# Two of six projection chunks computed as a 2x2 block product in seven products over pairs of rows

## The chip, the cores and the metric

The kernel runs on one core of a Trainium2 chip. The metric is the device time of one execution in microseconds, the median of several runs. The core's engines are named as in the profile: PE (TensorE, the matmuls), DVE (VectorE), ACT (ScalarE), POOL (GpSimd) and SP (SyncE, which here only issues DMA transfers). Each engine works through its own instructions in the order in which the kernel wrote them; a semaphore holds an instruction, and all behind it on that engine, until what it needs is there.

## The reference

Two mixers are computed from the same x (2048 rows of 1024) and blended by a gate. One is a local attention with 32 heads of 32, in which each position looks at eight positions, two apart; the other is a gated MLP with a product along the sequence.

```python
def reference(A_x, A_wqkv, A_wo, B_x, B_w_in, B_w_sp, B_b_sp, B_w_out, gate_w):
    x = A_x
    g = _sigmoid((x * gate_w).sum(-1, keepdims=True))
    a = _A_ref(x, A_wqkv, A_wo)                        # sliding, dilated attention
    b = _B_ref(x, B_w_in, B_w_sp, B_b_sp, B_w_out)     # gated MLP
    return g * a + (1 - g) * b

# _A_ref: qkv = x @ wqkv                      (1024 x 3072)
#         idx = pos - 2 * [0..7]; logits = q . k[idx] / sqrt(32), masked where idx < 0
#         a = (softmax(logits) . v[idx]) @ wo
# _B_ref: z = gelu(x @ w_in)                  (1024 x 3584), z1, z2 = its halves
#         z2 = layernorm(z2);  g = w_sp @ z2 + b_sp;  b = (z1 * g) @ w_out
```

Inputs and output are bfloat16.

## The kernel before

All work stands in one program order, written out by hand, under a manual schedule. PE's matmuls carry the time, and the other engines' work is put between them. A small planner (`Beat`) keeps a nominal clock, advanced by `beat.run(columns)` after every group of matmuls; `beat.at(t, fn)` puts other work into the program when the nominal clock reaches t, and the attention's DVE steps (`attention_steps(t)`) are drawn one after the other as the planner thinks DVE free. So the order on each engine is fixed when the program is built; only waits are decided on the chip.

The stages in order are:

- The first quarter of z2 (`z2_quad`, `z2_tile(i, 0)`), 128 rows by 512 columns at a time. Each tile is eight matmuls into one of eight PSUM banks, and ACT applies the gelu.
- The QKV projection. The weights' 24 blocks of 128 columns (8 groups of heads times q, k, v) make six chunks of four blocks (`wg_slots`, two slots in turn). Per chunk there are 16 "rows" j: row j holds the 128 positions p x 16 + j. A row is eight matmuls of 512 columns (`L520`), a copy of the bank by ACT (`L523`) and, for every four rows, four stores (`store_rows`, one per block) to q_d, k_d or v_d in DRAM. Chunk 0 is done as two halves of 256 columns. For blocks of v the weight columns are put in another order by ACT (`v_order`, `L269`, 1024 elements a partition). The loads of a chunk come a chunk ahead (`load_wg`).
- While PE works on the projection and what follows, DVE does the attention: per group a multiply of q by shifted k (`L326`, 8192 elements, twice a group), folds (`L329`, `L332` and so on), `soft_a`, the exponential on ACT (`soft_exp`, `L356`), `soft_b`, and the products with v (`L369` to `L376`).
- The rest of z2. The last of each row's tiles has one more column, the gate's weight, loaded at `L492`; the statistics and the norm of z2 and the gates follow.
- z1 (`L595`), then two chunks of the product along the sequence (`g_chunk`, `L613`), then the rest of it as 2x2 block products in seven products (`seven_products`, `L704`), which need sums of weight blocks (`t_sums`, `s_sum`).
- The output products (`mix_pair`, `attn_pair`, `both_pairs`), also in seven products.

The products in seven use f16 sums, and the factors are scaled by a power of two first, so that the sums fit. The power is found by `whole_power`: the largest absolute values (ACT's Abs with a sum on the way, or a DVE reduction) are rounded to a power on DVE and written to `top_b`; PE transposes this column to a row (`L557`); DVE reduces it to one number, `top_1`; PE spreads that over all partitions by a matmul (`L560`); six small DVE operations make the power and its inverse. Each `next(steps)` writes the part up to the next `yield`.

The projection's loop before is:

```python
    for ch in range(NCH):
        wgt = wg_slots[ch % 2]
        for pos0, pos1 in ((0, 2), (2, 4)) if ch == 0 else ((0, 4),):
            n0, n1 = pos0 * C, pos1 * C
            for j in range(NJ):
                if j == 4 and 0 < ch and ch + 1 < NCH:
                    load_wg(ch + 1)
...
                if j == 8 and pos1 == 4 and ch + 1 < NCH:
                    v_order(ch + 1)
```

Of the kernel before, what the change touches and what calls it, by code (L numbers as in the profile page):

```python
# [36 lines left out]
W2P = FH + 32  # L37
# [12 lines left out]
ARENA = EF_OFF + 15360  # L50
# [7 lines left out]
def kernel(  # L58
# [24 lines left out]
    def reg(off, n):  # L83
        return arena[:, off:off + n]
# [6 lines left out]
    wsp_d = dpool.tile([8, P, S], BF, name="wsp_d")  # L91
    wo_d = dpool.tile([NG, P, D], BF, name="wo_d")
# [4 lines left out]
    def warm_up(widths):  # L97
        pw = psum.tile([P, 512], F32, name="pw", tag="ps")
        for n in widths:
# [25 lines left out]
    v_l1 = sm.tile([P, 28], F32, name="v_l1")  # L125
# [9 lines left out]
    w_up = sm.tile([P, 1], I32, name="w_up")  # L135
    u_up = sm.tile([P, 1], I32, name="u_up")
# [19 lines left out]
    w2 = reg(CD_OFF, KT * W2P).rearrange("p (k c) -> p k c", k=KT)  # L156
    stage_slots = [reg(off, 2048).rearrange("p (j c) -> p j c", j=4)
                   for off in (CD_OFF + 14592, CD_OFF + 16640, EF_OFF + 13056)]
    wg_slots = [reg(EF_OFF + r * WGS, WGS).rearrange("p (t k c) -> p t k c", t=4, k=KT) for r in range(2)]
    vraw_slots = [reg(EF_OFF + 2 * WGS + r * KT * C, KT * C).rearrange("p (k c) -> p k c", k=KT) for r in range(3)]  # L160
    junk = reg(EF_OFF + 2 * WGS + 3 * KT * C, FH)
# [89 lines left out]
    def blocks(ch):  # L251
        return BLOCKS[4 * ch:4 * ch + 4]

    def load_w(ch, pos):
        g, part = blocks(ch)[pos]
        dst = vraw_slots[g % 3] if part == 2 else wg_slots[ch % 2][:, pos, :, :]
        sync.dma_start(dst, wq_v[:, :, part * D + g * C:part * D + (g + 1) * C])
# [5 lines left out]
    def v_order(ch):  # L263
        for pos, (g, part) in enumerate(blocks(ch)):
            if part != 2:
                continue
            vdst = wg_slots[ch % 2][:, pos, :, :].rearrange("p k (d h) -> p k d h", d=DH, h=HG)
            vsrc = vraw_slots[g % 3].rearrange("p k (h d) -> p k d h", h=HG, d=DH)
            nc.scalar.copy(vdst, vsrc)  # L269
# [9 lines left out]
    def z2_mm(ps, i, c, kt, N):  # L279
        nc.tensor.matmul(ps[:, 0:N], xT[:, kt, i * P:(i + 1) * P], w2[:, kt, ZC * c:ZC * c + N],  # L280
                         start=(kt == 0), stop=(kt == KT - 1))
# [100 lines left out]
    def load_v(g):  # L382
        sync.dma_start(v_t, bass.AP(tensor=v_d.tensor, offset=v_d.offset + (g * (S + 16) + 2) * C, ap=[[NJ * C, P], [1, NJJ * C]]))
# [10 lines left out]
    def attention_steps(t):  # L394
        beat.at(t - 8.0, lambda: load_qk(0))
        beat.at(t + 35.0, lambda: load_v(0))
# [75 lines left out]
    tc_order = ctx.enter_context(tc.manual_schedule())  # L472

    for i in range(2):
        sync.dma_start(xn[:, i, :], x_v[:, i, :])  # L475
    for c in range(2):
        sync.dma_start(w2[:, 0, ZC * c:ZC * (c + 1)], win_v[:, 0, FH + ZC * c:FH + ZC * (c + 1)])  # L477
    for kt in range(1, KT):
        sync.dma_start(w2[:, kt, 0:2 * ZC], win_v[:, kt, FH:FH + 2 * ZC])  # L479
    for i in range(2, 16):  # L480
        if i == 14:
            load_w(0, 0)
            load_w(0, 1)
        sync.dma_start_transpose(xT[:, :, i * P:(i + 1) * P], x2[i * P:(i + 1) * P, :])
    load_w(0, 2)
    load_w(0, 3)
    load_wg(1)
    for t_d in (k_d, v_d):
        sync.dma_start(bass.AP(tensor=t_d.tensor, offset=t_d.offset, ap=[[16, P], [(S + 16) * C, NG], [1, 16]]), zeros[:])
    for c in range(2, 4):  # L490
        sync.dma_start(w2[:, :, ZC * c:ZC * c + ZW[c]], win_v[:, :, FH + ZC * c:FH + ZC * c + ZW[c]])
    sync.dma_start(w2[:, :, FH:FH + 1], gw_v)  # L492

    warm_up((512,) * 6 + (128,))
    z2_quad()
    for i in range(2, 16):
        z2_tile(i, 0)

    QK_US = NJ * KT * 2 * C * BEAT
    beat.steps = attention_steps(beat.now + QK_US + 10.0)  # L500

    stg = 0
    def store_rows(st, ch, j0, pos0, pos1):
        for pos in range(pos0, pos1):
            g, part = blocks(ch)[pos]
            t_d, rows, first = ((q_d, S, 0), (k_d, S + 16, 16), (v_d, S + 16, 16))[part]
            dst = bass.AP(tensor=t_d.tensor, offset=t_d.offset + (g * rows + first + j0) * C, ap=[[NJ * C, P], [C, 4], [1, C]])
            sync.dma_start(dst, st[:, :, pos * C:(pos + 1) * C])

    for ch in range(NCH):  # L510
        wgt = wg_slots[ch % 2]
        for pos0, pos1 in ((0, 2), (2, 4)) if ch == 0 else ((0, 4),):
            n0, n1 = pos0 * C, pos1 * C
            for j in range(NJ):
                if j == 4 and 0 < ch and ch + 1 < NCH:
                    load_wg(ch + 1)
                ps = psum.tile([P, 512], F32, name="ps", tag="ps")
                for kt in range(KT):
                    lhsT = _sub_ap(xT_flat, kt * S + j, [[NJ, P]])
                    nc.tensor.matmul(ps[:, n0:n1].rearrange("p (t c) -> p t c", c=C), lhsT, wgt[:, pos0:pos1, kt, :],  # L520
                                     start=(kt == 0), stop=(kt == KT - 1))
                st = stage_slots[stg % 3]
                nc.scalar.copy(st[:, j % 4, n0:n1], ps[:, n0:n1])  # L523
                if j % 4 == 3:
                    store_rows(st, ch, j - 3, pos0, pos1)
                    stg += 1
                if j == 8 and pos1 == 4 and ch + 1 < NCH:
                    v_order(ch + 1)
                beat.run(KT * (n1 - n0))

    load_w1(0)
    load_w1(1)
    sync.dma_start(b_row[:], bass.AP(tensor=B_b_sp.tensor, offset=B_b_sp.offset + 1024, ap=[[P, 8], [1, P]]))
    for i in range(16):
        for c in range(2 if i < 2 else 1, 4):
            z2_tile(i, c)
        nc.scalar.activation(junk.rearrange("p (f q) -> p f q", q=P), z2[:, :, i, :], ACT.Square, accum_out=s2[:, i:i + 1])
        if i % 4 == 3:
            beat.at(beat.now + 6.0, lambda i=i: stats(i))
            for ii in range(i - 3, i + 1):  # L540
                beat.at(beat.now + 11.0, lambda ii=ii: norm(ii))
    beat.at(beat.now + 8.0, gates)
    for aa in range(4):
        beat.at(beat.now + 8.0 + 6.0 * aa, lambda aa=aa: load_wsp(0, aa))
    beat.at(beat.now + 6.0, lambda: sync.dma_start(
        bsp_bc[:, 0:1024], bass.AP(tensor=B_b_sp.tensor, offset=B_b_sp.offset, ap=[[0, P], [1, 1024]])))

    def whole_power(up1, factors):
# [19 lines left out]
        yield  # L568

# [424 lines left out]
    def extra(n, place):  # L994
# [14 lines left out]
        if n == 5 and place == 0:  # L1009
            nc.vector.tensor_reduce(top[:], v_l1[:], AX.X, ALU.max)  # L1010
            next(v_steps)
# [102 lines left out]
```

## Time and profile before

| what | value |
|---|---|
| median of 3 runs | 691.0 us (690.73 to 691.04) |
| the profiled execution | 691.45 us, of which the span is 689.4 |
| PE busy | 683.3 us, 99% of the span |
| DVE, ACT busy | 530.3 us (77%), 385.9 us (56%) |
| first quarter of z2 | to 38.35 us |
| projection, L520 | 38.35 to 204.44 us, 896 matmuls |
| rest of z2 | to 270.30 us |
| z1 | to 367.00 us |
| g_chunk, twice | to 465.50 us |
| seven_products | to 551.60 us |
| granted TensorE clock | 1.000 |

The times of the stages are those of PE in the profiled execution, counted from the start of the span. A group of the profile is named by its line in the kernel, engine, operation and tiles, with the count of its instructions, their busy time and the mean duration of one, and then the idle time of the engine ahead of them with what ended it. Matmuls overlap, so that the time from one to the next is shorter than the duration of one. In a timeline each row has its start, its duration, and in brackets the idle time of that engine before it. PE is idle for about 6 us in all, none of it in the projection.

### The profile page before, as it was taken

What the parts mean: (1) busy time and instruction counts of PE and PEld (TensorE: products, weight loads), DVE (VectorE), ACT (ScalarE), POOL (GpSimd) and SP (SyncE); (2) the same over time, 40 slices, a digit from 0 to 9 for tenths busy, and PEclk for the clock granted to TensorE, in tenths of its full rate; (3) what the DMA queues carried; (4) which work ended last, traced back from release to release, by engine and by line L of the source; (5) the groups of instructions that cost most, each with busy time, mean ns of one, the idle gap of its engine ahead of it and who ended that gap; (6) DMA issues with size and microseconds to landing.
All of it is one profiled execution on the core that took longest, in us unless ns stands there. A gap on an engine that the chain in (4) does not pass through costs nothing.

```text
span 689.4 us, 9052 instructions
## 1 busy us (share of the span) xinstructions
PE 683.3 (99%) x3355; PEld 359.1 (52%) x3355; DVE 530.3 (77%) x685; ACT 385.9 (56%) x778; POOL 12.6 (2%) x44
## 2 busy tenths in 40 slices
PE   8999999999999999999999999999999999999998
PEld 3489666666665555444444444444444444444443
DVE  0003779999999999999999887276589998766653
ACT  4345444345458898764675987853665552222332
POOL 0000000000000111000000000000000000000000
PEclk9999999999999999999999999999999999999999
DMA  8996769678856213998988938937112433222210
GB/s 225 181 217 171 145 196 229 129 168 194 200 159 200 88 58 117 245 214 295 320 264 224 356 128 195 245 95 267 39 32 62 128 56 86 68 62 61 70 54 30
DMA packets 186411, 108.14 MB, mean 157 GB/s; under 512 B 145920, under 2 KB 171008, under 8 KB 186112
## 3 DMA queue, kind: packets, MB, share of 16 engines
q1 hardware_dynamic: 184064, 99.18, 55.1%
q10 hardware_dynamic: 2304, 8.39, 3.1%
q8 instruction: 26, 0.43, 0.2%
q14 instruction: 17, 0.14, 0.1%
HBM read 59.25 MB, written 34.15 MB: 135 GB/s over the span
## 4 chain that ended last, share of the span: by engine, by line
PE 98%; DMA 1%; SPq 0%; ACT 0%; DVE 0%; issue 0%; DVEq 0%
PE ps L520 24%; PE ps L613 14%; PE ps L595 14%; PE ps L280 14%; PE ps L704 12%; PE ps L830 12%; PE ps L919 6%; PE ps L909 1%; DMA arena<-in_B_w_in_dram 1%; PE po L560 0%; SPq L477 0%; SPq L475 0%; PE po L557 0%; ACT arena L973 0%; DVE arena L899 0%; SPq L479 0%
## 5 line engine op out<-in xcount | busy, mean ns | idle before, releaser
L520 PE MATMUL ps<-arena 128*128 128x512 bf16 (+1 forms) x896 | 166.2, 349 | 0.0
L520 PEld LDWEIGHTS <-arena 128*128 128x128 bf16 x896 | 120.2, 144 | 45.9
L326 DVE TENSOR_TENSOR arena<-arena 128x8192 bf16<-128x8192 bf16 x16 | 70.8, 4422 | 57.4 <-DMA arena<-k_d 57.2
L523 ACT CAST arena<-ps 128x512 bf16<-128x512 f32 (+1 forms) x112 | 57.7, 526 | 85.2 <-PE ps L520 79.5
L280 PE MATMUL ps<-arena 128*128 128x512 bf16 (+1 forms) x512 | 97.6, 352 | 2.1 <-DMA arena<-in_B_w_in_dram 2.1
L613 PE MATMUL ps<-arena 128*128 128x512 bf16 x448 | 97.7, 379 | 0.0
L595 PE MATMUL ps<-arena 128*128 128x512 bf16 x448 | 96.9, 379 | 0.0
L830 PE MATMUL ps<-arena 128*128 128x512 f16 (+1 forms) x392 | 92.8, 379 | 0.0
L704 PE MATMUL ps<-arena 128*128 128x512 bf16 (+1 forms) x392 | 85.5, 379 | 0.0
L280 PEld LDWEIGHTS <-arena 128*128 128x128 bf16 x512 | 50.1, 98 | 49.3 <-issue 2.7
L369 DVE TENSOR_TENSOR arena<-arena,att_A 128x8192 bf16<-128x8192 bf16 x16 | 70.7, 4419 | 2.7 <-DMA arena<-v_d 2.7
L595 PEld LDWEIGHTS <-arena 128*128 128x128 bf16 x448 | 43.8, 98 | 52.7
L613 PEld LDWEIGHTS <-arena 128*128 128x128 bf16 x448 | 43.3, 98 | 52.3 <-issue 0.7
L830 PEld LDWEIGHTS <-arena 128*128 128x128 f16 (+1 forms) x392 | 38.3, 98 | 46.1
L704 PEld LDWEIGHTS <-arena 128*128 128x128 bf16 (+1 forms) x392 | 38.0, 98 | 45.9 <-issue 0.5
L329 DVE TENSOR_TENSOR arena<-arena 128x4096 bf16<-128x4096 bf16 (+1 forms) x32 | 56.2, 1758 | 1.0
L919 PE MATMUL ps<-arena 128*128 128x512 f16 (+3 forms) x200 | 50.3, 375 | 0.0
L285 ACT ACTIVATE arena<-ps 128x512 bf16<-128x512 f32 (+1 forms) x64 | 34.3, 538 | 28.3 <-PE ps L280 28.3
L899 DVE SCALAR_TENSOR_TENSOR arena<-ps,g_s,arena 128x512 bf16<-128x512 f32 (+2 forms) x33 | 23.9, 733 | 28.5 <-ACT arena L951 20.0
L598 ACT ACTIVATE arena<-ps 128x512 bf16<-128x512 f32 x56 | 30.7, 596 | 17.3 <-DMA z_d<-arena 11.6
L375 DVE TENSOR_TENSOR arena<-arena 128x4096 bf16<-128x4096 bf16 x16 | 36.6, 2289 | 0.3
L919 PEld LDWEIGHTS <-arena 128*128 128x128 f16 (+1 forms) x200 | 19.4, 98 | 23.1 <-issue 0.2
(169 smaller groups left out, 624.0 us busy)
## 6 DMA issues: line engine op xcount, KB each, us to landing
arena<-k_d SPq DMA_DIRECT2D x8, 960.0 KB, 6.5
arena<-v_d SPq DMA_DIRECT2D x8, 960.0 KB, 9.3
arena<-in_A_wqkv_dram SPq DMA_DIRECT2D x24, 256.0 KB, 4.5
z_d<-arena SPq DMA_DIRECT2D x12, 512.0 KB, 7.5
arena<-in_B_w_in_dram SPq DMA_DIRECT2D x4, 1024.0 KB, 7.5
q_d<-arena SPq DMA_DIRECT2D x32, 128.0 KB, 2.7
k_d<-arena SPq DMA_DIRECT2D x32, 128.0 KB, 2.4
arena<-q_d SPq DMA_DIRECT2D x8, 512.0 KB, 4.3
```

The lines of the kernel that those rows point to most:

```text
L280: nc.tensor.matmul(ps[:, 0:N], xT[:, kt, i * P:(i + 1) * P], w2[:, kt, ZC * c:ZC * c + N], start=(kt == 0), stop=(kt == KT - 1))
L326: TT(prod.rearrange("p (w j c) -> p w j c", w=W, j=8, c=C), in0, in1, ALU.mult)
L329: return lambda: TT(pv[:, :, 0:half], pv[:, :, 0:half], pv[:, :, half:2 * half], ALU.add)
L369: TT(prod.rearrange("p (w j d h) -> p w j d h", w=W, j=8, d=DH, h=HG), in0, in1, ALU.mult)
L375: return [(4.4, mul), (2.3, lambda: TT(p3[:, 0:4, :], p3[:, 0:4, :], p3[:, 4:8, :], ALU.add)), (1.2, lambda: TT(p3[:, 0:2, :], p3[:, 0:2, ...
L520: nc.tensor.matmul(ps[:, n0:n1].rearrange("p (t c) -> p t c", c=C), lhsT, wgt[:, pos0:pos1, kt, :], start=(kt == 0), stop=(kt == KT - 1))
L523: nc.scalar.copy(st[:, j % 4, n0:n1], ps[:, n0:n1])
L595: nc.tensor.matmul(ps[:], w1[:, kt, (f % 4) * P:(f % 4 + 1) * P], xT[:, kt, 512 * c:512 * (c + 1)], start=(kt == 0), stop=(kt == KT - 1))
L613: nc.tensor.matmul(ps[:], z2[:, f, i, :], wsp[:, i, :, :].rearrange("p a t -> p (a t)"), start=(i == 0), stop=(i == 15))
L704: nc.tensor.matmul(dst[:], lhs[:, k, :], rhs(k), start=first and k == 0, stop=k == 7, skip_group_check=not first)
L830: nc.tensor.matmul(dst[:], lhs[:, j, :], rhs(j), start=first and j == 0, stop=j == 6, skip_group_check=not first)
L919: nc.tensor.matmul(dst, lhs[:, k, :], rhs[:, k, :], start=first and k == 0, stop=k == 3, skip_group_check=not first)
```

## The change

Chunks 3 and 4 (eight blocks, 1024 columns) are taken together as a 2x2 block product: the two block rows of x are the positions of rows j = 2m and 2m + 1, the inner dimension is halved (four tiles of 128 each), and the weight's halves are b11, b21 (chunk 3) and b12, b22 (chunk 4). `row_pair(m, ...)` makes two rows of both chunks in seven products of four matmuls (28 instead of 32), in Winograd's form, with the partial sums held in PSUM, copied from bank to bank by ACT, and joined by two DVE operations a pair. Between its products stand the eight matmuls of one row of chunk 5 in three parts (`plain_rows(5, m, 0, 4, 2, 3)`). The order of the chunks becomes 0, 1, 2, the eight pairs with rows 0 to 7 of chunk 5, rows 8 to 15 of chunk 5.

The sums that this needs are made as follows.

- Sums of x: `x_sum` finds the largest absolute values of x on DVE during the first quarter of z2; `x_steps` (a `whole_power`) is put at rows 3 and 6 of the first half of chunk 0; `x_block_sums` at row 7 makes `a22s` on ACT and five arrays of 4096 elements on DVE, ahead of the attention, in the part of z2's memory that isn't yet written. The second row block of z2's tiles that lies there is stored to `z2_d` and loaded again after the pairs.
- Sums of the weights: the loads of chunks 3, 4 and 2 are issued after chunk 0, chunk 5's after chunk 1. In chunk 1 ACT finds the weights' sizes (`q_abs`, 16 Abs of 512 elements, rows 5 to 12) and reorders v blocks (rows 4, 7, 9); `q_first_step` is at row 14, and the other two steps of `q_steps` at rows 0 and 2 of chunk 2. There follow `q_scale` (rows 3 to 6, ACT), `v_order(5)` (row 7), four `q_sum` (row 9, DVE) and two scalings by the power of x (rows 11 and 12).

Chunk 2's weights lie where w2's first quarter was, so the loads of w2's last two quarters, of the gate column and the loading of z2 from `z2_d` come after the pairs. The attention is planned 3 us later (13.0 in place of 10.0 behind the first half of chunk 0), and `t_sums` and `s_sum` 4 us earlier. A pair's rows are stored two at a time, in place of four.

The diff, cut to its core:

```diff
+    def x_sum(i):
+        v = xn[:, i, :] if i < 2 else xT[:, :, i * P:(i + 1) * P]
+        nc.vector.tensor_reduce(x_l1[:, i:i + 1], v, AX.X if i < 2 else AX.XY, ALU.max,
+                                apply_absolute_value=True)
...
+    def x_block_sums():
+        v = nc.vector
+        nc.scalar.activation(a22s, x_block(1, 1), ACT.Copy, scale=x_by)
+        v.tensor_scalar(a21s, x_block(0, 1), x_by, None, ALU.mult)
+        TT(x_sums[0], a22s, a21s, ALU.add)
+        v.scalar_tensor_tensor(x_sums[2], x_block(0, 0), x_by, a21s, ALU.mult, ALU.subtract)
+        v.scalar_tensor_tensor(x_sums[1], x_block(0, 0), x_by, x_sums[0], ALU.mult, ALU.subtract)
+        v.scalar_tensor_tensor(x_sums[3], x_block(1, 0), x_by, x_sums[1], ALU.mult, ALU.add)
+
+    def q_abs(k):
+        slot = wg_slots[3 + k // 8]
+        nc.scalar.activation(abs_out.rearrange("p (k c) -> p k c", k=4), slot[:, k % 8 // 2, 4 * (k % 2):4 * (k % 2) + 4, :],
+                             ACT.Abs, accum_out=q_l1[:, k:k + 1])
+
+    def q_scale(ch, h, up1):
+        v = wg_slots[ch][:, 2 * h:2 * h + 2]
+        nc.scalar.activation(v, v, ACT.Copy, scale=up1[:].bitcast(F32))
...
+    def q_first_step():
+        nc.vector.tensor_reduce(top[:], q_l1, AX.X, ALU.max)
+        next(q_steps)
...
-    beat.steps = attention_steps(beat.now + QK_US + 10.0)
+    beat.steps = attention_steps(beat.now + QK_US + 13.0)
...
+    def row_pair(m, filler):
...
+        pa = bank()
+        mm(pa, plain(0), b11, True)
+        pb = bank()
+        nc.scalar.copy(pb[:], pa[:])
+        pe = bank()
+        mm(pe, summed(x_sums[0]), t_w[0], True)
+        act(e5, pe[:], ACT.Copy, scale=back1)
+        next(filler)
+        mm(pb, summed(x_sums[1]), t_w[1], False)
+        pc = bank()
+        nc.scalar.copy(pc[:], pb[:])
+        mm(pa, plain(1), b21, False)
+        act(st3[:, 0, :], pa[:], ACT.Copy, scale=back1)
+        next(filler)
+        mm(pb, summed(x_sums[2]), t3_w, False)
+        pd = bank()
+        nc.scalar.copy(pd[:], pb[:])
+        stt(st4[:, 1, :], pb[:], back1, e5, ALU.mult, ALU.add)
+        beat.on_vector(0.75)
+        mm(pc, summed(x_sums[3]), b22, False)
+        stt(st4[:, 0, :], pc[:], back1, e5, ALU.mult, ALU.add)
+        beat.on_vector(0.75)
+        next(filler)
+        mm(pd, lambda k: a22s[:, k, m:1024:8], t_w[2], False)
+        act(st3[:, 1, :], pd[:], ACT.Copy, scale=back1)
+        for st, ch in ((st3, 3), (st4, 4)):
+            store_rows(st, ch, j, 2, 0, 4)
...
+    for pos0, pos1 in ((0, 2), (2, 4)):
+        for j in range(NJ):
+            if pos0 == 0 and j in (3, 6):
+                next(x_steps)
+            if pos0 == 0 and j == 7:
+                x_block_sums()
+            if pos0 == 2 and j == 2:
+                v_order(1)
+            run_all(plain_rows(0, j, pos0, pos1))
+    for ch in (3, 4, 2):
+        load_wg(ch)
+    for j in range(NJ):
+        if j in (4, 7, 9):
+            v_order({4: 3, 7: 4, 9: 2}[j])
+        if 5 <= j < 13:
+            q_abs(2 * j - 10)
+            q_abs(2 * j - 9)
+        if j == 14:
+            q_first_step()
+        run_all(plain_rows(1, j, 0, 4))
+    load_wg(5)
+    for j in range(NJ):
+        if j in (0, 2):
+            next(q_steps)
+        if 3 <= j < 7:
+            q_scale(3 + (j - 3) // 2, (j - 3) % 2, q_up)
+        if j == 7:
+            v_order(5)
+        if j == 9:
+            for k in range(4):
+                q_sum(k)
+        if j in (11, 12):
+            q_scale(3, j - 11, x_up)
+        run_all(plain_rows(2, j, 0, 4))
+    for m in range(8):
+        row_pair(m, plain_rows(5, m, 0, 4, 2, 3))
+    for c in (2, 3):
+        sync.dma_start(w2[c][:, :, 0:ZW[c]], win_v[:, :, FH + ZC * c:FH + ZC * c + ZW[c]])
+    sync.dma_start(w2[3][:, :, 256:257], gw_v)
+    sync.dma_start(z2[:, 4:8, 0:2, :], z2_d[:])
+    stg[0] = 0
+    for j in range(8, NJ):
+        run_all(plain_rows(5, j, 0, 4))
...
-        beat.at(t0 + 82.0 + 2.5 * k, lambda k=k: t_sums(k))
+        beat.at(t0 + 78.0 + 2.5 * k, lambda k=k: t_sums(k))
...
-        beat.at(t0 + 87.0 + 0.8 * k, lambda k=k: s_sum(0, k))
+        beat.at(t0 + 83.0 + 0.8 * k, lambda k=k: s_sum(0, k))
```

In the changed kernel `whole_power`'s transpose is L498 and its matmul L501, and the projection's matmuls are L612 (rows) and L632 (pairs).

More of the change, by code (lines that the diff above doesn't have):

```diff
@@ L500 @@
-    beat.steps = attention_steps(beat.now + QK_US + 10.0)
[L502 to L546, printed above, removed]
     def whole_power(up1, factors):
@@ new lines, with x_block @@
+    for i in range(2, 16):
+        x_sum(i)
+        z2_tile(i, 0)
+        if i == 8:
+            sync.dma_start(z2_d[:], z2[:, 4:8, 0:2, :])
+    nc.vector.tensor_reduce(top[:], x_l1, AX.X, ALU.max)
+    x_steps = whole_power(x_up, q_back[:])
+    next(x_steps)
+    x_by = x_up[:].bitcast(F32)
+    def x_block(half, e):
+        return x_even_odd[:, 4 * half:4 * half + 4, :, e]
+    def x_block_sums():
[6 more added lines that the diff above has]
+        v.scalar_tensor_tensor(x_sums[3], x_block(1, 0), x_by, x_sums[1], ALU.mult, ALU.add)
@@ L1009, in extra @@
         if n == 5 and place == 0:
-            nc.vector.tensor_reduce(top[:], v_l1[:], AX.X, ALU.max)
+            nc.vector.tensor_reduce(top[:], v_l1, AX.X, ALU.max)
             next(v_steps)
```

169 lines of the change are left out of this document (130 added, 39 removed).

## The prediction

> **What bounds the kernel now.** I read the page's busy times, the chain that ended last and the groups first. PE is busy for 99% of the span and the chain is PE; L520, the projection that is changed, is its largest line, and PE never waits for another engine in it.
>
> ```profile
> PE 683.3 (99%) x3355; PEld 359.1 (52%) x3355; DVE 530.3 (77%) x685; ACT 385.9 (56%) x778; POOL 12.6 (2%) x44
> PE 98%; DMA 1%; SPq 0%; ACT 0%; DVE 0%; issue 0%; DVEq 0%
> L520 PE MATMUL ps<-arena 128*128 128x512 bf16 (+1 forms) x896 | 166.2, 349 | 0.0
> L523 ACT CAST arena<-ps 128x512 bf16<-128x512 f32 (+1 forms) x112 | 57.7, 526 | 85.2 <-PE ps L520 79.5
> ```
>
> So a matmul less is a gain at full price, and a wait of PE a loss at full price. Next the timeline of ACT over the second chunk (columns: start, duration, engine, line, operation, count, idle before):
>
> ```profile
> 76.75 0.58 ACT L523 CAST arena<-ps 128x512 bf16<-128x512 f32 x1 [1.15 <-PE ps L520]
> 78.48 0.58 ACT L523 CAST arena<-ps 128x512 bf16<-128x512 f32 x1 [1.14 <-PE ps L520]
> ...
> 82.41 3.85 ACT L269 COPY arena<-arena 128x1024 bf16<-128x1024 bf16 x2
> 86.12 1.60 ACT L523 CAST arena<-ps 128x512 bf16<-128x512 f32 x3
> 87.73 1.28 ACT L356 ACT_TABLE_LOAD   x1
> 89.03 0.63 ACT L356 ACTIVATE att_L<-att_L 128x512 f32<-128x512 f32 x1
> ```
>
> Row copies come every 1.7255 us (mean over the rows), so one of the row's 8 matmuls takes 215.7 ns. A copy behind other work holds ACT 0.485, one v_order 1.92. For each row ACT has 1.14 us free and no more. The price of an Abs with its sum is 0.755 from start to start, 0.70 to a copy behind it, in a later stage of the same timeline:
>
> ```profile
> 381.55 0.63 ACT L633 ACTIVATE arena<-arena 128x512 bf16<-128x512 bf16 x1
> 382.08 0.19 ACT L633 ACTIVATION_READ_ACCUMULATOR arena<-arena 128x1 f32 x1
> 382.31 0.63 ACT L633 ACTIVATE arena<-arena 128x512 bf16<-128x512 bf16 x1
> ```
>
> DVE around the first softmax, where it waits for ACT once:
>
> ```profile
> 89.69 0.42 DVE L347 TENSOR_TENSOR att_m<-att_L 128x256 f32<-128x256 f32 x1 [6.26 <-ACT att_L L356]
> ...
> 91.94 4.42 DVE L326 TENSOR_TENSOR arena<-arena 128x8192 bf16<-128x8192 bf16 x1
> 96.39 2.29 DVE L329 TENSOR_TENSOR arena<-arena 128x4096 bf16<-128x4096 bf16 x1
> ```
>
> And PE: what a broadcast matmul and a transpose of whole_power cost it between others, and the start of the kernel:
>
> ```profile
> 0.77 2.83 PE L100 MATMUL pw<-const-bfloat16-1.0 128*128 128x512 bf16 x7 [0.77 <-PEq L1098]
> 3.38 1.35 PE L296 MATMUL pt<-ident,arena 128*128 128x128 bf16 x16
> ...
> 401.94 0.38 PE L560 MATMUL po<-top,const-bfloat16-1.0 1*128 1x512 bf16 x1
> 402.26 1.04 PE L613 MATMUL ps<-arena 128*128 128x512 bf16 x4
> ```
>
> The profiled execution took 691.45 us, its span 689.4; the median of the runs is 691.0. My terms are differences on its timeline, and I add them to the median.
>
> **Saving.** Sixteen rows of two chunks were 256 matmuls; eight pairs of 7 products of 4 are 224. 32 x 215.7 ns = -6.90 us. The f16 products are priced like bf16: both have a mean of 379 ns in their groups.
>
> **Added on PE.** Two whole_powers. The matmul costs 402.26 - 401.94 = 0.32; a transpose at 498.42 had the next matmul at 498.57, 0.15. Together +0.94. The first one's parts are before chunk 1 (+0.47).
>
> **The x part.** Sixteen tensor_reduce on DVE lie beside the first z2 tiles, where DVE is idle (its first multiply is at 62.25); I take them as hidden: the transpose is two us behind the last. x_block_sums starts near 45; its ACT half, 4096 elements, is 3.7 us at the rate of L670 (2048 in 2.0, contiguous) or 7.7 at L269's (1024 in 1.92, strided), against eight banks of 0.873 us = 7.0. So 0 to 1.3; I take 0, as the banks have part of it free.
>
> **Chunk 1, the main term.** All of q_abs (16 Abs) and v_order(3), (4) and twice (2) now stand in ACT's order in rows 4 to 12 of chunk 1. Row 3's copy starts at 73.30 + 0.47 = 73.77 and frees ACT at 74.25. Behind it: v_order(3) 1.92, the copy of row 4 0.485, eight times two Abs (0.755 + 0.70) with seven copies (0.485) between, 15.0, v_order(4) 1.92, v_order(2) 3.84: 23.2 us, in which nothing waits. The last Abs ends at A = 97.4. PE, which has eight banks, isn't held (the copies lag by 8 us, under five rows), and ends chunk 1 at 94.3 (the z2 tiles end at 38.35; 32 rows of 256 columns at 0.873 make 66.3, 16 rows at 1.7255 make 93.9, and 0.47). There next(q_steps) sets the transpose L498 in its order, which needs top_b, and this needs the last Abs, the reduce (row of L558: 0.27) and four tiny DVE ops at 0.19: 98.6. **PE idles 4.3.** Behind it two rows (0.15 + 3.45) bring PE to L501 at 102.2, which needs top_1. DVE's order, which the two programs' instruction lists show, puts ahead of that reduce the softmax's second half and the next QK multiply. ACT: copy of row 12 0.49, table load 1.28, exponential 0.65, 99.85; DVE: 2.25 (89.69 to 91.94) and 4.45, 106.55; reduce 0.27 and passing on, 107.0. **PE idles 4.8 more.** Sum +9.1. The second end hangs on A alone, so the sum is A + 9.6 (107.0 - 97.4) less 97.9 (when PE would have come there unhindered, 94.3 + 3.6). It is zero if A is 88.3, and gives back just the saving at A of about 94. I put A within a microsecond: every duration in it has a row of the same shape, save that the operand of v_order and Abs lies elsewhere.
>
> By the trace's granted clock, 1.000 in every stage, such idle time costs nothing beyond itself; but no idle time there is over 1.35 us. The start shows a slow array: six matmuls of 512 and one of 128 take 3.38 - 0.77 = 2.61 us, 0.42 per 512, twice 0.2157. The Trainium skill (TensorE: Matmul & The Clock Gate, "HAM oscillation — how this bites in real kernels") says that idle gaps over about 3.4 us put the array back to half rate, for about as long once it works again; no idle time in this trace is long enough to show it. By it the second gap would cost an estimated 1.7 more, the first nothing, since the second's end is DVE's.
>
> **Chunk 2 and the pairs.** q_scale (4 x 2.0 on ACT, as L670), v_order(5) 3.84, two scalings 4.0 and 16 copies come to 20 us beside 27.6 of PE; q_sums 4 x 1.22 lie on DVE before the pairs. A pair takes 36 x 0.2157 = 7.77 us; ACT has five operations and a copy of 0.5 to 0.7 in it, DVE two of 0.75. A DVE operation behind a 4.45 multiply is late by that much, and its bank is wanted 5.4 later at the soonest. Pair 0 stages where chunk 2's last rows are still being stored: +0.4 (0 to 1). Twice as many stores, 0.45 each to issue, make 4.5 of 7.77 on SP's queue: hidden.
>
> **The gate column.** It and w2's last half are loaded only after the last pair's stores. With E the end of the pairs: last DVE sum E + 3.0 (it may stand behind a multiply), four stores, w2's chunks issued at E + 5.2 and E + 6.0, the second landing 7.5 later, and the gate load, which writes into its rows, starts after it: E + 13.5, issue 1.41 (42.12 before), landing 2 (stores 2.4; loads up to 4.3), E + 16.9. The tile that uses it is due at E + 8 x 1.7255 + 1.73 = E + 15.5. +1.4 (0 to 4).
>
> **DVE later on.** It is 10.2 us late after the softmax, has 12 + 4.9 of new work, some 2.5 of tiny ops and 2 of waits in the pairs, less the 5 that PE is late by then: some 27. In the stretch of the g chunks (367.0 to 465.5) the view by windows has DVE busy for 72.56 of 98.5, so it is idle for 26, of which 23 lie ahead of t_sums(2). That ends at 475.3 for a product due at 473.9: +1.5 (0 to 4).
>
> **Sum.** -6.90 + 0.94 + 9.1 + 0.4 + 1.4 + 1.5 = +6.4: 697.4.
>
> **Rivals.**
> 1. Faster: ACT is through early. If Abs and v_order run faster in parallel than one behind the other, or PE reaches the steps later, the waits vanish; with the late terms at zero, -6.9 + 0.9 = 685.0, up to 688 with them. It decides at A of 88 to 94. Against it: ACT's 23.2 us between 74.25 and the transpose at 94.3 would have to take 9 less for A to be 88.3, and every row of it comes from operations that already stood one behind the other. That the change does less than it says, because its products over strided f16 sums run slower than 215.7 ns, would only add time, and I give it no chance of its own. Chance 0.15.
> 2. One wait only: the top_1 reduce slips in ahead of the multiply, or A is 2 to 3 earlier: 690 to 694. Against it is DVE's order. 0.13.
> 3. The array slows after the second gap. For the price, the start's slow stretch lasted 2.6 us at least and ended by 6.08, 5.3 at most: half is lost, 1.3 to 2.7, 699.4. No row decides for or against. 0.12.
> 4. The late stage is worse: the pairs' DVE operations come behind 4.4-us multiplies time after time, gate and t_sums at the upper ends: 700 to 705. 0.10.
> 5. The forecast, 695 to 699.5: 0.50.
>
> **Numbers.** Predicted 697.4. From 689.5 to 702 lie the forecast, rivals 2 and 3 and half of 4, eight in ten. A measurement tells 0.2%, 1.4 us, from no change. Faster by that is rival 1 with its sum: 0.16; within, the low end of rival 2: 0.05; slower 0.79.
>
> **What would show it.** Right: in the profile after, 4.3 us of PE idle before L498 released by DVE top_b, and 4.8 before L501 by top_1, at about 94 and 102; ACT without idle time from 74 to 97; pairs of 7.77; PE idle about 1.4 before a z2 tile for the gate DMA. Wrong: no idle before L498 and L501 (A is misjudged), or a slow row of matmuls behind them (rival 3), or the largest waits in the pairs or at L704's successor (rival 4).

## The result, and the profile after

The changed kernel takes 723.6 us (median of six runs, 719.93 to 732.83) against 690.87 before, a ratio of 1.0464 with a 95% interval of 1.0427 to 1.0501. Slower was forecast, but 6.4 us, not 33. One of the six, 732.83, is a slow run, which the ratio leaves out. The profiled execution took 719.93, the least of the six; its span is 717.7. Against the 691.45 of the profiled execution before, that is 28.5 us of loss, and not the medians' 33.

The page of the changed kernel, its busy times, the granted clock by slices, the chain and the projection's two groups:

```profile
PE 686.9 (96%) x3327; PEld 355.6 (50%) x3327; DVE 583.7 (81%) x752; ACT 422.5 (59%) x835; POOL 14.4 (2%) x45
PEclk9999989999999999999999999998899999999999
PE 66%; ACT 10%; DVE 7%; DMA 7%; SPq 6%; issue 3%; ACTq 0%; DVEq 0%
L612 PE MATMUL ps<-arena 128*128 128x512 bf16 (+1 forms) x640 | 118.9, 342 | 0.0
L632 PE MATMUL ps<-arena 128*128 128x512 f16 (+1 forms) x224 | 52.4, 379 | 3.9 <-ACT ps L663 3.3
```

There are 32 matmuls of the projection less, as meant. But PE's part of the chain has fallen from 98% to 66%, and two places of the clock's row show 8 where all were 9. The waits of PE (what waits, for what, us in sum, times, longest) name the places:

```profile
PE ps L874 <- ACT ps L896: 5.7, 1, 5.7
PE ps L874 <- DVE arena L852: 4.9, 1, 4.9
PE ps L765 <- ACT arena L768: 3.7, 3, 1.8
PE ps L632 <- ACT ps L663: 3.3, 1, 3.3
PE po L498 <- DVE top_b L494: 3.3, 1, 3.3
PE po L501 <- DVE top L499: 3.2, 1, 3.2
PE ps L297 <- DMA arena<-in_gate_w_dram: 1.1, 1, 1.1
```

L498, L501 and the gate column were forecast. By stage, from the start and end of PE's groups (before: rows times 1.7255 within the projection):

| stage | before | after | difference |
|---|---|---|---|
| to the end of z2's first quarter | 38.35 | 37.1 | -1.3 |
| chunks 0 and 1 | 55.5 | 56.4 | +0.9 |
| chunk 2 | 27.6 | 38.5 | +10.9 |
| the other three chunks | 82.9 | 79.6 | -3.3 |
| rest of z2 | 65.9 | 67.5 | +1.6 |
| z1 | 96.7 | 100.9 | +4.2 |
| g chunks | 98.5 | 98.5 | 0 |
| seven_products | 86.1 | 100.9 | +14.8 |
| output products to the end | 137.8 | 138.3 | +0.5 |

Chunk 2 is what the prediction said. In the timelines of ACT and DVE the queue of chunk 1 ends, and the steps follow in the order that was worked out:

```profile
95.05 0.63 ACT L564 ACTIVATE arena<-arena 128x512 bf16<-128x512 bf16 x1
...
97.55 0.63 ACT L373 ACTIVATE att_L<-att_L 128x512 f32<-128x512 f32 x1
```

```profile
95.80 0.17 DVE L589 TENSOR_REDUCE top<-o_l 128x1 f32<-128x16 f32 x1 [10.90 <-ACT arena L564]
...
100.46 4.42 DVE L343 TENSOR_TENSOR arena<-arena 128x8192 bf16<-128x8192 bf16 x1
104.79 0.27 DVE L499 TENSOR_REDUCE top<-po 1x1 bf16<-1x128 bf16 x1
```

The last Abs ends at 95.67 (97.4 was forecast, on a timeline that starts 1.3 later), DVE stands 10.9 for it, and the reduction to one number stands behind the multiply. What wasn't counted on is the clock. The view by windows (columns: window, length, busy time and count of PE, PEld, DVE, ACT and POOL, granted clock, DMA share, GB/s) behind the first, second, t_sums(2)'s and the Abs' wait:

```profile
96.00:98.00 2.00, 1.22 (x4) 0.60 (x5) 0.61 (x4) 1.97 (x3) 0.00 (x0) 0.55 0.86 192
108.00:110.00 2.00, 2.00 (x7) 0.81 (x6) 1.93 (x4) 1.80 (x2) 0.00 (x0) 0.54 0.92 301
490.00:492.00 2.00, 2.00 (x6) 0.74 (x5) 0.69 (x1) 0.57 (x1) 0.00 (x0) 0.50 0.84 241
520.00:522.00 2.00, 2.00 (x6) 0.76 (x5) 0.00 (x0) 0.11 (x1) 0.00 (x0) 0.50 0.00 0
```

In the last three of these rows PE is busy all through and makes six or seven matmuls in 2 us, where ten or eleven are counted in such a row at a granted clock of 1.00.

The two waits in seven_products are the largest part. At the first, t2 was made late by DVE, whose attention ended at 484.1 in place of 424.7. At the second, in seven_products(2), the copy that opens the second product stands in ACT's order behind eight Abs over the attention's output, 6.0 us of them, from 513.11 on:

```profile
518.39 0.63 ACT L407 ACTIVATE arena<-arena 128x512 bf16<-128x512 bf16 x1
518.92 0.19 ACT L407 ACTIVATION_READ_ACCUMULATOR arena<-arena 128x1 f32 x1
519.02 0.58 ACT L896 COPY ps<-ps 128x512 f32<-128x512 f32 x1
```

In the kernel before, these Abs are in the g chunks. The planner puts them there: they are due some 15 us after its own end of the attention, which the change moves from 412 to 448 on the planner's clock (worked out from the code); that clock is flushed only between two seven_products, so all eight fell on one spot. The reduction of the sums of all such Abs (L1185, at 512.85) now stands ahead of these eight, so the power that it gives doesn't rest on them.

### The profile page after: what moved, and what is told of

Read it like the earlier page. It is cut to its first block, busy times and chain, and to the rows that moved or that the text cites. A ratio compares the mean times of both kernels' runs of the same rounds, so it can differ in the third digit from the quotient of the medians.

```text
span 717.7 us, 9166 instructions
## 1 busy us (share of the span) xinstructions
PE 686.9 (96%) x3327; PEld 355.6 (50%) x3327; DVE 583.7 (81%) x752; ACT 422.5 (59%) x835; POOL 14.4 (2%) x45
## 4 chain that ended last, share of the span: by engine, by line
PE 66%; ACT 10%; DVE 7%; DMA 7%; SPq 6%; issue 3%; ACTq 0%; DVEq 0%
PE ps L297 13%; PE ps L1000 12%; PE ps L874 11%; PE ps L612 10%; PE ps L632 6%; PE ps L1089 6%; PE ps L765 4%; SPq L484 3%; PE ps L783 3%; DMA arena<-in_B_w_out_dram 2%; ACT arena L803 2%; DMA arena<-in_B_w_in_dram 2%; ACT arena L286 1%; ACT arena L407 1%; DMA v_d<-arena 1%
## 5 line engine op out<-in xcount | busy, mean ns | idle before, releaser
L612 PE MATMUL ps<-arena 128*128 128x512 bf16 (+1 forms) x640 | 118.9, 342 | 0.0
L612 PEld LDWEIGHTS <-arena 128*128 128x128 bf16 x640 | 83.4, 145 | 33.8 <-issue 7.3
L297 PE MATMUL ps<-arena 128*128 128x512 bf16 (+1 forms) x512 | 98.2, 353 | 1.9 <-DMA arena<-in_gate_w_dram 1.1
L874 PE MATMUL ps<-arena 128*128 128x512 bf16 (+1 forms) x392 | 89.8, 392 | 10.6 <-ACT ps L896 5.7
L1000 PE MATMUL ps<-arena 128*128 128x512 f16 (+1 forms) x392 | 92.8, 379 | 0.0
L297 PEld LDWEIGHTS <-arena 128*128 128x128 bf16 x512 | 49.9, 98 | 49.8 <-DMA arena<-in_gate_w_dram 1.6
L765 PEld LDWEIGHTS <-arena 128*128 128x128 bf16 x448 | 43.8, 98 | 56.9 <-issue 4.5
L783 PEld LDWEIGHTS <-arena 128*128 128x128 bf16 x448 | 43.3, 98 | 52.3 <-issue 0.7
L1000 PEld LDWEIGHTS <-arena 128*128 128x128 f16 (+1 forms) x392 | 38.2, 98 | 46.1
L618 ACT CAST arena<-ps 128x512 bf16<-128x512 f32 (+1 forms) x80 | 38.0, 503 | 38.0 <-PE ps L612 37.9
L632 PE MATMUL ps<-arena 128*128 128x512 f16 (+1 forms) x224 | 52.4, 379 | 3.9 <-ACT ps L663 3.3
L1069 DVE SCALAR_TENSOR_TENSOR arena<-ps,g_s,arena 128x512 bf16<-128x512 f32 (+2 forms) x33 | 23.9, 733 | 28.5 <-ACT arena L1121 19.9
L632 PEld LDWEIGHTS <-arena 128*128 128x128 f16 (+1 forms) x224 | 32.3, 144 | 20.4 <-issue 4.6
```

The source lines that it names most:

```text
L618: nc.scalar.copy(slot[:, j % 4, n0:n1], ps[:, n0:n1])
L632: nc.tensor.matmul(dst[:].rearrange("p (t c) -> p t c", c=C), lhs(k), rhs[:, :, k, :], start=first and k == 0, stop=k == 3, skip_group_che ...
L765: nc.tensor.matmul(ps[:], w1[:, kt, (f % 4) * P:(f % 4 + 1) * P], xT[:, kt, 512 * c:512 * (c + 1)], start=(kt == 0), stop=(kt == KT - 1))
L783: nc.tensor.matmul(ps[:], z2[:, f, i, :], wsp[:, i, :, :].rearrange("p a t -> p (a t)"), start=(i == 0), stop=(i == 15))
L874: nc.tensor.matmul(dst[:], lhs[:, k, :], rhs(k), start=first and k == 0, stop=k == 7, skip_group_check=not first)
L1000: nc.tensor.matmul(dst[:], lhs[:, j, :], rhs(j), start=first and j == 0, stop=j == 6, skip_group_check=not first)
```

## The experiments

Line numbers of these kernels differ a little from the changed kernel's.

**PE kept busy in the waits** (e1). Are the slow stretches a cost of their own?

```diff
+            keep_busy(14 if j == 0 else 19)     # matmuls over constants, ahead of next(q_steps)
             next(q_steps)
...
+        if n in (0, 2):
+            keep_busy(21 if n == 0 else 25)
         product(pb, sums[1], lambda k: t2[:, k], False)
```

> The changed kernel, in whose four longest waits PE no longer stands still: 14 idle-time matmuls of 512 columns (over constants, into a bank that nobody reads) ahead of the transpose of q_steps, 19 ahead of its matmul, 21 ahead of the third product of seven_products(0) and 25 ahead of that of seven_products(2). They cost 0.216 us each at the full clock, so they fit into the waits. If the waits alone cost the time, nothing changes: 719.9 us, span 717.7. If each long wait also sets the array to half rate for some time after it, the granted clock stays at 1.00 behind all four, and the time falls by what the slow stretches cost: about 1.9 behind the second wait, 2.7 and 1.9 behind the other two, nothing behind the first (its end is followed by a wait that DVE ends): 713 to 714.

Measured: 718.42 (716.47 to 719.84, four runs), the profiled one 719.84. The same stretch as above and the product that needs t2:

```profile
108.00:110.00 2.00, 2.00 (x11) 1.34 (x10) 1.96 (x3) 2.00 (x2) 0.00 (x0) 1.00 1.27 294
490.00:492.00 2.00, 1.61 (x9) 0.57 (x7) 1.97 (x4) 0.00 (x0) 0.00 (x0) 1.00 0.99 290
```

```profile
491.06 24.35 PE L880 MATMUL ps<-arena 128*128 128x512 f16 x112 [0.39 <-DVE arena L858]
```

The clock stayed at 1.00 behind all four waits: the slow array follows from PE standing still, that is shown. By the medians 5.2 us were won; the two profiled executions are alike (719.84 and 719.93). In chunk 2, 1.2 us were won (the pairs begin at 130.76 in place of 131.95, behind a wait of 1.2 for a scaling). But two other waits of PE now had a slow array behind them, that of the first pair (3.2; the changed kernel's 3.3 had 1.00 behind it) and one in z1 (3.5, where the changed kernel has 1.8 at most):

```profile
142.00:144.00 2.00, 2.00 (x6) 0.82 (x5) 2.00 (x3) 0.69 (x1) 0.00 (x0) 0.50 0.00 0
338.00:340.00 2.00, 2.00 (x7) 0.64 (x5) 2.00 (x1) 1.97 (x6) 0.00 (x0) 0.50 1.02 281
```

Some 6 us of work each ran at about half rate there, an estimated 2.9 and 2.8 lost. So PE came to seven_products 3.9 later (482.47 and 478.60), and the product that needs t2 began 3.9 later too. From the start of seven_products to the end this kernel takes 235.2 against 239.1, 3.9 less: the price of the two slow stretches there.

**A fixed power** (e2).

```diff
+    nc.gpsimd.memset(q_back[:], 2.0 ** -7)
+    nc.gpsimd.memset(q_up[:].bitcast(F32), 2.0 ** 7)
...
-            q_abs(2 * j - 10)
-            q_abs(2 * j - 9)
...
-            q_first_step()
...
-            next(q_steps)
```

> The changed kernel without the search for the weights' power: no Abs in chunk 1, no reduction, no transpose and matmul of q_steps; the power that this search finds for these inputs is put in as a constant, everything else stays. Theory (the lateness starts in chunk 1's ACT queue): both waits in chunk 2 are gone (chunk 2 takes 27.6 to 29 us in place of 38.5), the first exponential comes near 89 in place of 97.5, so DVE and the attention are 9 us earlier against the same PE, the waits of z1 and that of 4.9 in seven_products(0) shrink to under 2 each; the wait behind eight Abs in seven_products(2) stays, since the planner's clock places it: about 700. Rival (the later waits come from DVE's added work alone): 709 to 710, with the wait of seven_products(0) at 4 or more.

Measured: 714.15 (711.84 to 721.46), 9.5 less than the changed kernel by the medians; the profiled execution, 721.46, is the longest of the four. In it the waits in chunk 2 were gone, and the pairs began at 121.7, 10.2 earlier. But t2's product began at 488.27, after a wait of 8.0, DVE having stood 6.2 for a load of v: neither theory. There the 10 us of the projection's waits were lost again ahead of t2. In the three shorter executions they were not, or not all; no profile of these was kept.

**The Abs spread** (e3).

```diff
-        beat.at(t + 14.0, lambda: store_o(NG - 1))
+        beat.at(t + 1.0, lambda: store_o(NG - 1))
...
+        if n == 0 and place > 2:
+            for k in range(3 * place - 9, min(8, 3 * place - 6)):
+                o_abs(NG - 1, k)
```

> The changed kernel with one thing moved: the last store of the attention's output is due 1 us after the attention's planned end in place of 14, and the eight Abs over it stand in seven_products(0) behind its fourth to sixth places, two or three at a time, in place of all eight ahead of seven_products(2). Theory (ACT's copy that opens the second product stands behind eight Abs): the 5.7 us wait of PE in seven_products(2) goes and with it the slow array behind it, 1.9: 712 to 713. Rival (the Abs hold ACT wherever they are): PE waits as long in seven_products(0) or (1): 718 to 720.

Measured: 721.76 (714.21 to 729.50), no answer by the time. In the profiled execution (721.84) the wait of 5.7 and its slow stretch were gone, and a wait of 1.0 came in seven_products(1); but t2's product waited 9.7, DVE having stood 5.5 for a load of v. So the moved Abs free PE at that place, as the theory had it; the time met neither expectation.

**The reordering later** (e7), the test of the prediction's main term.

```diff
-        if j in (4, 7, 9):
-            v_order({4: 3, 7: 4, 9: 2}[j])
+        if j in (4, 9):
+            v_order({4: 3, 9: 2}[j])
...
+        if j == 1:
+            v_order(4)                          # in chunk 2
```

> The changed kernel with the reordering of chunk 4's v block moved from row 7 of chunk 1 to row 1 of chunk 2 (1.92 us of ACT); its Abs read the block as it was loaded. Theory (both waits in chunk 2 hang on the end of the last Abs): the last Abs ends 1.9 earlier (95.67 in the changed kernel), the transpose starts near 94.9 in place of 96.78 and the matmul near 103.2 in place of 105.12, with a wait left of about 1.4 before the transpose, and 3 before the matmul. Rival (they hang on DVE's queue): the transpose or the matmul stays within 0.5 of its old time. The total says little here: 716 to 722.

One profiled run, 731.23. PE's two steps:

```profile
95.12 0.22 PE L498 MATMUL po<-ident,top_b 128*1 128x128 bf16 x1 [1.43 <-DVE top_b L494]
103.46 0.37 PE L501 MATMUL po<-top,const-bfloat16-1.0 1*128 1x512 bf16 x1 [4.51 <-DVE top L499]
```

Both come 1.66 earlier (96.78 and 105.12 before the edit), in an execution whose first quarter of z2 ended 0.2 later: 1.9 earlier for the 1.92 that was moved, as the theory has it. The chain from the last Abs is shown. The first wait is 1.4, as expected; the second is 4.5 and not 3, since the clock stays at 1.00 behind the short first wait and PE comes sooner to the second.

**Less work for DVE** (e6). Sixteen operations of DVE, group 3's products with v, are left out, so that group's output isn't computed. The planner still counts their time, so everything else stays in its place.

```diff
-                    yield t, took, fn           # in pv_steps(g - 1, 0) and (g - 1, 1)
+                    yield t, took, fn if g != 4 else (lambda: None)
```

> The changed kernel with DVE's sixteen operations of one group's products with v left out (group 3, some 17 us of DVE; its output columns are those of another group); nothing else is moved. Theory (from chunk 2 to seven_products(0) DVE is the bound, and PE's wait there is DVE's lateness): the wait of 4.9 at t_sums(2)'s product goes, and the slow array behind it: 7.6 less than the changed kernel's profiled 719.9, 712 to 713, while the waits in chunk 2 and behind the eight Abs stay as they are. Rival (the wait hangs on t2's place or on ACT): 4 us or more are left of it and the time is 718 or more.

Measured: 725.30 (722.45 to 727.73), not less. DVE's timeline from the end of z2 into z1:

```profile
280.92 0.17 DVE L460 TENSOR_REDUCE mean<-s 128x4 f32<-128x16 f32 x1 [5.20 <-ACT arena L302]
...
289.78 0.17 DVE L475 TENSOR_SCALAR g_s<-omg 128x16 f32<-128x16 f32 x1 [6.67 <-ACT omg L474]
...
334.35 0.69 DVE L389 TENSOR_TENSOR arena<-arena 128x1024 bf16<-128x1024 bf16 x1 [10.86 <-ACT arena L407]
350.06 0.42 DVE L364 TENSOR_TENSOR att_m<-att_L 128x256 f32<-128x256 f32 x1 [4.66 <-ACT att_L L373]
```

The theory fell. The 17 us became waits, most of which the fence shows: for z2's last tiles, for the gates, for the Abs that free the attention's output, for an exponential. DVE's waits of over 0.9 between 130 us and t2 sum to 39.9, against 17.5 in the changed kernel, and t2's product began 3.8 later. So DVE isn't late by its load. Its order ties it to ACT, and to PE through ACT, until z1; it is late by what it waits for there and behind, where the plan leaves it 4 us (448 to 451 on the planner's clock).

**The late stages alone** (e9): the loads of q, k and v a few us later, the Abs over the loads of w_out 3 us later, those over the attention's output 3 earlier, the last eight spread, t2's product fourth; the program of the projection's own work is that of the changed kernel. The diff shows three of these moves.

```diff
-                beat.at(t + 1.0, lambda g=g: load_qk(g + 1))
+                beat.at(t + (6.0 if g else 1.0), lambda g=g: load_qk(g + 1))
...
-                    beat.at(t + 1.0, lambda g=g: load_v(g))
+                    beat.at(t + 3.0, lambda g=g: load_v(g))
...
-        beat.at(beat.now + 9.5 + 7.0 * k, lambda total=total, slot=slot: nc.scalar.activation(
+        beat.at(beat.now + 12.5 + 7.0 * k, lambda total=total, slot=slot: nc.scalar.activation(
```

> The changed kernel with its projection as it is, waits in chunk 2 included, and only the later stages mended: loads of q, k and v a few us later (group 1's as they were), the Abs over w_out's loads 3 us later and those over the attention's output 3 earlier, the last eight of these spread over seven_products(0), t2's product fourth. Theory (what is lost behind the projection is lost to ACT's and SP's order, not to DVE's added work): the 3.7 of PE in z1, the 4.9 + 2.7 at t_sums(2)'s product and the 5.7 + 1.9 behind the Abs all shrink, 12 to 19 in sum: 701 to 708. Rival (DVE's load and the lateness from chunk 2 decide): the wait at that product stays at 4 or more, only the Abs' part goes: 711 to 714.

Measured: 703.43 (702.21 to 705.70), ratio 1.0149 (1.0077 to 1.0222): 20 us less than the changed kernel by the medians (14 by the profiled executions), with its waits in chunk 2 still there (3.3 and 1.6). The wait at the first pair (3.3) was gone with the later loads. In z1 PE didn't wait; DVE's waits from 130 us on sum to 11.7, 5.8 less, and t2's product began at 481.65, 5.5 earlier. A wait of 5.1 stayed at it, as PE was earlier too. So the loss behind chunk 2 lay mostly in the order of ACT and SP; which move brought how much wasn't tried.

**The rows first** (e4): chunk 5's last rows ahead of the pairs, so that the weights' sums have 13.8 us more.

```diff
+    for j in range(8, NJ):                      # ahead of the pairs
+        if j == 8:
+            for k in range(4):
+                q_sum(k)
+        if j in (12, 13):
+            q_scale(3, j - 12, x_up)
+        run_all(plain_rows(5, j, 0, 4, 2 if j < 12 else 1))
     for m in range(8):
         row_pair(m, plain_rows(5, m, 0, 4, 2, 3))
...
+    for i in range(2, 16):
+        z2_tile(i, 1)
```

> A version that should remove every wait: rows 8 to 15 of chunk 5 stand ahead of the pairs (13.8 us more room for the weights' sums), half of the Abs comes after the first exponential, the reorderings of chunks 3 and 4 move to chunk 2, the steps of q_steps to rows 6 and 9 of chunk 2, the scalings to rows 11 to 14, the sums and the two scalings by the power of x into the rows of chunk 5; the tiles of z2's second quarter come first after the pairs, so that w2's loads and the gate column have 24 us; the last eight Abs as in the run before. Theory: PE has no wait over 1 us in the projection and in z2; the attention is 20 to 24 us later than in the kernel before, against 26 us that DVE was idle in the g chunks, so seven_products(0) waits 0 to 3: 685 to 689. Rival (DVE's added work is too much in any order): the wait ahead of t_sums(2)'s product stays at 4 to 5, with a slow array behind it: 691 to 694.

Measured: 700.81 (699.89 to 701.83), ratio 1.0123 (1.0066 to 1.0180). No wait in chunk 2 and none for the gate column; 2.4 were left before the first pair and 6.0 at t2's product, with a slow stretch behind it: the rival's wait, in a time above both expectations.

**Waits taken out one by one** (e5, e8, e10), each from the profile of the one before.

```diff
+            beat.at(t + (1.0 if g else -3.0), soft_exp)         # e5, with e9's moves, load_v at t + 6.0
+                beat.at(t + 6.0, lambda g=g: load_qk(g + 1))    # e5
...
+                beat.at(t + (6.0 if g else 1.0), lambda g=g: load_qk(g + 1))   # e8, load_v at t + 3.0, exp at -5.0
...
-    for ch in (3, 4, 2):                                        # e10
-        load_wg(ch)
+    load_wg(3)
+        if j in (3, 7):
+            load_wg({3: 2, 7: 4}[j])
+        beat.at(t0 + (83.0 + 0.8 * k if k < 2 else 96.5), lambda k=k: s_sum(0, k))
```

> The version with the rows first, with what its profile still shows taken out: the first exponential stands two rows earlier on ACT (DVE waited 6.0 for it), the sums of the weights stand one row earlier (PE waited 2.4 at the first pair), the loads of q, k and v are due 6 us after DVE is done with the buffer in place of 1 (SP stood before them, and the loads behind them held ACT for up to 5.8 in z1), the Abs over the loads of w_out are due 3 us later, those over the attention's output 3 us earlier; in seven_products(0) the product that needs t2 comes fourth in place of third (1.73 more room), and there are no Abs of z1 in it. Theory: every us that DVE doesn't wait shows as a us less at t_sums(2)'s product, which waited 6.0 with 2.6 of slow array behind it; with 2.4, 1.5 and 1.0 of other waits the sum is 13 less at best: 687 to 690 by median, from 700.8. Rival (DVE's load, not its waits, decides): the wait at that product stays over 3 us and the time is 694 to 698.

Measured: 695.29, ratio 1.0052 (1.0015 to 1.0090). The wait of 6.0 fell to 3.2, but a move of its own cost as much, in DVE's timeline:

```profile
98.72 4.42 DVE L343 TENSOR_TENSOR arena<-arena 128x8192 bf16<-128x8192 bf16 x1 [7.05 <-DMA arena<-k_d]
```

Group 1 has no products with v ahead of it, and so no cover for a later k.

> The version before, mended where its profile shows new waits: group 1's q and k are loaded at the old time (DVE stood 7.05 for k, and PE 2.2 and 1.0 for q_steps behind it), v 2 us after DVE is done rather than 5 (DVE stood 3.5), and the first exponential stands ahead of one reordering (DVE still waited 4.2). Theory (the wait at t_sums(2)'s product is the sum of DVE's earlier waits less what the planner leaves free): DVE gains 7 + 3.5 + 2.5, so that product's wait of 3.2 with 1.5 to 2 of slow array behind it goes, and the 3.2 in chunk 2 too: 695.3 less 8 is 687 to 688, faster than the kernel before by 0.4%. Rival (waits move on: DVE is held again by ACT or a load in z1 and g): 2 us or more stay at that product and the time is 690 to 693.

Measured: 691.69, ratio 0.9961 (0.9920 to 1.0002), not told from the kernel before. t2's product began at 467.63 in place of 471.58, 3.95 earlier, for 4.6 us less of DVE's waits; 2.9 were still waited there, as the rival said. The eight pairs took 62.2 us.

> The version before with three moves. The twelve loads of weights behind chunk 0 are put in three places (chunk 3's there, chunk 2's at row 3, chunk 4's at row 7 of chunk 1): as one block they took SP 13.4 us to issue, and group 1's k, which stands behind them, came 3.7 us after DVE wanted it. Two of the four sums of seven_products(0) and the last small operations of wo's power, 2.6 us of DVE, stand behind t_sums(2) in place of ahead of it. Theory (that product's wait is DVE's backlog of 6 us at the end of the g chunks, and each us of DVE's earlier waits is in it): the backlog falls by 3.7 + 2.6, the wait of 2.9 and the slow array behind it go: 4 us less than 691.7, 687 to 688.5. Rival (DVE is held again by another load before): 1.5 us or more of that wait stay, 689.5 to 691.5.

Measured: 689.20 (688.48 to 689.75, eleven runs), ratio 0.9971 (0.9952 to 0.9991): faster than the kernel before, by 1.4 us by the medians; its longest run is below the shortest of that kernel's beside it (689.86). Its page and the timeline of PE at t2's product:

```profile
PE 678.6 (99%) x3327; PEld 354.5 (52%) x3327; DVE 583.7 (85%) x752; ACT 422.1 (61%) x835; POOL 11.2 (2%) x45
```

```profile
465.23 1.89 PE L888 MATMUL ps<-arena 128*128 128x512 f16 x8 [0.54 <-DVE arena L866]
467.78 3.61 PE L888 MATMUL ps<-arena 128*128 128x512 f16 x16 [0.66 <-ACT ps L921]
472.57 2.75 PE L888 MATMUL ps<-arena 128*128 128x512 f16 x12 [1.19 <-DVE arena L932]
```

The wait is 0.5 and the clock 1.00 throughout. Only half of the reason held: DVE waited as long for group 1's k as before (4.2, and 3.7 in e8), and the gain is that of the 2.6 us of DVE's work moved behind t_sums(2); 1.2 of it came back as a wait three products later.

## Why the prediction was wrong, step by step

- **The saving** held. The projection of e10, with no wait in it, takes 160.7 against 166.1 (from its first matmul to the first of z2's next tiles: 37.09 to 197.81, and 38.19 to 204.27): -5.4, where -6.9 + 0.9 was worked out. A pair is 62.2 / 8 = 7.77, as was said.
- **The x part** held: no wait of PE; its ACT half took 3.73, the contiguous row's rate, though its operand is strided.
- **Chunk 1, the main term,** held: the mechanism, the order and the end (L501 at 105.12; 107.0 less the 1.3 of the start is 105.7). The two idle times were 3.3 and 3.2, not 4.3 and 4.8: on the forecast's timeline the last Abs ended 0.4 sooner and PE ended chunk 1 0.5 later, and the array was slow between the two waits, so that PE came later to the second.
- **The clock** was priced rightly and counted wrongly. By the view by windows the array was slow for some 3.4 us of work behind the second wait and for 5.0 and 3.2 in seven_products; half of it is lost, 1.7, 2.5 and 1.6, within rival 3's 1.3 to 2.7 per gap. It had 0.12 and one gap; there were four, and gaps of 3.2 and 3.3 were enough. Yet 3.3 at the first pair was not (the clock is 1.00 behind it). The other runs are mixed too: waits of 2.4 (e2, at 474.3), 2.9 (e8) and 3.0 (e3, first pair) brought a clock of about 0.5, while 2.9 in z1 (e6), 3.0 in z1 (e7) and 3.3 in chunk 2 (e3) did not; every wait of 3.5 or more did. By the Trainium skill (TensorE: Matmul & The Clock Gate, "HAM oscillation — how this bites in real kernels") idle gaps over about 3.4 us bring it; the runs agree above that, but below it the length alone doesn't decide, and what does stays open.
- **The first pair** was mis-sized: 3.3 for 0 to 1. ACT's copy stood 5.3 for the store of chunk 2's last v rows, which SP issued behind two loads of the attention; the step had counted the stores alone. In e9, with these loads behind the stores, the copy stood 1.95 and PE didn't wait.
- **The gate column** held: 1.06 for 1.4.
- **DVE later on** is the step that failed. It set 27 us of added work against 23 of idle time, as if work and idle time could be moved against each other. e6 shows that in this order they can't: 17 us of work less made nothing earlier. What counts is DVE's waits from z1 on. Those of the changed kernel from 130 us to t2 are, first of all (columns as above), these two, both in z1:

```profile
DVE arena L389 <- ACT arena L407: 7.6, 1, 7.6
DVE att_m L364 <- ACT att_L L373: 4.6, 1, 4.6
```

e9 shows that they come of the order of ACT and SP: with loads and Abs moved there, the first is gone and the second is 0.8. That ACT and SP stand on loads and Abs because the planner placed them by a clock that, worked out from the code, has PE at the end of the g chunks 27 us earlier than the chip (7 in the kernel before), is argued from the two clocks and wasn't tried by itself. The term was 1.5; it measured 4.9 and 2.5 of slow array.

- **What was not in the sum at all**: the eight Abs behind the planner's later end of the attention (5.7 and 1.6), and z1 (4.2). The prediction followed DVE alone into the late stages; every `beat.at` that hangs on the attention's time had moved with it, on ACT and on SP.

What these terms measured beyond the forecast, 1.7 behind the second wait, 2.9 at the first pair, 5.9 at t2's product, 7.3 behind the Abs and 4.2 in z1, comes to 22.0, and the profiled execution lies 22.1 above the forecast (28.5 less 6.4); the small differences that are left cancel.

What stays open is the spread. In the profiles of e2, e3, e6 and e7 DVE stands 4.5 to 6.2 for a load of v in the g chunks and t2's product waits 7.1 to 9.7; in those of e9 and of the changed kernel it doesn't, and the wait is 5. That this is why the changed kernel's runs range over 7 us and more, and why its median lies 3.7 above the profiled execution, was not tried.

## What to carry to other kernels

Where one engine is busy for 99% and its order is fixed, a step that it must wait for is paid in full, and where the step held PE for some 3 us or more, a slow stretch behind it mostly cost 1.4 to 2.9 on top. Added work on an engine with idle time is not paid out of that idle time: find the first place where this engine must be on time, and add up what it waits for ahead of it. When a planner places work by a nominal clock, list everything that hangs on a moved time, on every queue, and not only the operations that the diff names.

## What the hardware showed that was not expected

- Four idle times of 3.2 to 5.7 us of PE were followed by a granted clock of 0.50 to 0.60 for some 3 to 5 us of work; in e1, with matmuls in these gaps, it stayed at 1.00 behind them. Between 2.4 and 3.3 us some waits had it and some had not.
- Twelve loads of 256 KB in a row held SP for 13.4 us (67.5 to 81.0 in e8), 1.1 each, where four in the kernel before took 0.8 to 0.9 each. In e10, where they were to be spread, eight still stood in a row (9.4 us), and the load behind them didn't come sooner to DVE.
